# A linear-attention and feed-forward kernel on one core: w to the 128th as one Exp, A in pairs, three quarters of w_in issued together, and a new written-out order

## The chip, the cores and the metric

The kernel runs on one core of one Trainium2 chip. A core has a matrix engine (TensorE, PE in the profile), a vector engine (VectorE, DVE), a scalar engine (ScalarE, ACT), a general engine (GpSimd, POOL) and a queue engine (SyncE, SP) that here only issues DMAs. Each engine runs its own instructions in the order in which they were issued and waits on semaphores for the others. The metric is device time in microseconds (us): 180.36 before, the median of three runs (180.33, 180.36, 181.3).

## The reference

Two layers. The first is a linear attention with a state, over 4 batches, 8 heads, 768 steps and a head size of 48:

```python
for t in range(S):
    cur = einsum('bhd,bhe->bhde', u * k[t], v[t])
    y[t] = einsum('bhd,bhde->bhe', r[t], state + cur)
    state = w * state + einsum('bhd,bhe->bhde', k[t], v[t])
```

w is between 0.85 and 0.95. The second takes x, the y of all heads side by side (3072 rows of 384), through two matrices and a smooth gate:

```python
h = x @ w_in                                   # 384 -> 2048
g = where(h >= 1, h, where(h <= -1, 0, (h + 1)**2 / 4))
out = g @ w_out                                # 2048 -> 384
```

## The kernel before

**Groups.** The 768 steps are cut into 6 chunks of 128. A group g is one chunk of two batches (256 rows of x), so there are 12 groups: g = 0 and 1 are chunk 0 of batches 0,1 and 2,3, and so on. A number n = 2g + j is one batch of a group. Loads of R and K for group 0 are cut into half loads by batch (0.0 and 0.1); the others are whole (384 KB).

**Attention, per group.** Within a chunk the recurrence becomes matrix products. R is scaled by powers of w (`Rs`, line 255), K by inverse powers (`Ks`, 257); `KU` = K u (259), `RKU` = R KU (261), and the sum of RKU over a head is `diag` (274). These four products are named Rs, Ks, KU, RKU with the group's number, the sum usum. V is cast to bf16 (`V`, 140) and `V2` = V diag (279, steps V20.0 and V20.1 for the halves of group 0, V21.0 for group 1 and so on). Per batch: T and TT transpose Rs and Ks on TensorE and copy them out (320, 140; groups 0 to 3), later groups use transposing DMAs (RT, KT, 405). A (331) multiplies them, 8 matmuls with 48 rows each; it takes two of four PSUM banks, and VectorE masks each bank into AT (336, two steps). Y (353, 358) multiplies AT by V and adds the state's part; y (366) adds V2. Sp (343) is the state's new term; Tm (374, 376), decay (379) and sbf (140) bring the state on, with `wCm`, w to the 128th spread over a tile. X and xT transpose y (387, 140; later by DMA, 424).

**Feed-forward, per group.** q runs over four quarters of the 2048 columns. mm1 (459) makes hp = x w_in for a quarter; relu (470 on ScalarE, 472 on VectorE), square (480 on ScalarE, 482 on GpSimd) and gate (489, VectorE) make gt; mm2 (514) multiplies gt by a quarter of w_out into op; o copies op out (140) and out stores it (532). In group 0 a quarter is cut into two halves of 512 columns in three small PSUM buffers; from group 1 on hp has two large ones, in the same banks, which are free once all of group 0's gates are done.

**The powers of w.** ScalarE loads a table for Ln (line 91), takes lw = Ln(w) (146), loads a table for Exp (191); TensorE spreads lw over all partitions (150), and two Exps make the factors Wup and Wdn (166, 169). For wCm, TensorE turns w into a column (wc, 157), VectorE copies it out (174, w_take), GpSimd squares it seven times (178, w_power) and ScalarE spreads it (180, wCm).

**Weights.** w_in and w_out come as four quarters each, cast to bf16 on the way, issued from GpSimd (209); a name with "!" is the issue. The first, w_in0!, is held until R of group 1 has landed, by a one-word copy (208). Everything else is issued by SyncE, on one queue.

**What sets the order.** The program text `PLAN` lists every step once, by name; "/1" takes the second of the engines that the step may run on, "@" gives the PSUM banks, "+n" puts n matmuls ahead of it whose result nobody reads (543, "warm" in the profile). The steps are issued in that order, so each engine runs its own in that order, and GpSimd and SyncE wait in line likewise.

Of the kernel before, what the change touches and what calls it, by code (L numbers as in the profile page):

```python
# [9 lines left out]
F32 = mybir.dt.float32  # L10
# [13 lines left out]
def kernel(  # L24
# [55 lines left out]
    w_col = const.tile([P, NP], F32, name="w_col")  # L80
# [6 lines left out]
    nc.vector.memset(w_col, 1.0)  # L87
# [3 lines left out]
    nc.scalar.preload_act_table_set("natural_log")  # L91
# [33 lines left out]
    FINE = 1  # L125
# [4 lines left out]
    def op(name, where, fn):  # L130
        ops[name] = (where, fn)
# [39 lines left out]
    def w_take(e):  # L171
        for j in range(2):
            rows = slice(j * HP, j * HP + D)
            nc.vector.tensor_copy(w_col[rows, :], tiles["wc"][rows, :])

    def w_power(e):
        for _ in range(C.bit_length() - 1):
            engines[e].tensor_mul(w_col, w_col, w_col)  # L178
# [12 lines left out]
    op("exps", ("ACT",), lambda e: nc.scalar.preload_act_table_set("exp_and_others"))  # L191
    op("Wup", ("ACT",), wup)
    op("Wdn", ("ACT",), wdn)
    op("w_take", ("DVE",), w_take)
    op("w_power", ("POOL", "DVE",), w_power)
# [27 lines left out]
    for g in range(nG):  # L223
# [3 lines left out]
        for j0, j1 in parts:  # L227
# [57 lines left out]
            op(f"V2{tag}", ("POOL", "DVE",) if early_g else ("POOL",), u_term)  # L285
# [23 lines left out]
        for j in range(UNITS):  # L309
# [99 lines left out]
            op(f"A{n}", ("PE",), a_mm)  # L409
# [24 lines left out]
        for q in range(nQ):  # L434
# [6 lines left out]
            for x, (f0, f1) in enumerate(runs):  # L441
# [32 lines left out]
                def square(e, g=g, q=q, x=x, f0=f0, f1=f1):  # L474
# [6 lines left out]
                    elif scale == 1.0:  # L481
                        nc.gpsimd.tensor_mul(sq, pt, pt)  # L482
                    else:
                        nc.gpsimd.scalar_tensor_tensor(out=sq, in0=pt, scalar=0.25, in1=pt, op0=ALU.mult, op1=ALU.mult)
# [17 lines left out]
                op(f"relu {mx}", ("ACT", "DVE",), relu)  # L502
                op(f"square {mx}", ("ACT", "POOL",), square)
# [35 lines left out]
    def fill(n):  # L539
# [9 lines left out]
        RKU0.1/1; load R2.0; X0@3+8; wc@1; Ks1.0/1; xT0; usum0.1; T2@0; w_in1; AT1.1; T3@3; V20.1; TT2; Y1@2; TT3/1; KU1.0;  # L549
        y1; A2@03+3; w_take; X1@2; mm1 (0, 0)00@0; AT2.0; xT1; w_in2; RKU1.0; AT2.1; mm1 (0, 0)01+2; mm1 (0, 1)00@1;  # L550
        relu (0, 0)0/1; mm1 (0, 1)01; mm1 (0, 1)10@2; square (0, 0)0; Sp1@1; V1/1; usum1.0; mm1 (0, 1)11; relu (0, 1)0;
        A3@02; w_in3; Sp0@3; square (0, 1)0; gate (0, 0)0; w_power; relu (0, 1)1; AT3.0; mm1 (0, 2)00@0+5; square (0, 1)1;
        mm1 (0, 2)01; gate (0, 1)0; Y2@0; relu (0, 2)0; mm1 (0, 2)10@1; gate (0, 1)1; load K2.0; mm1 (0, 2)11; AT3.1;
        square (0, 2)0; V21.0; relu (0, 2)1; Y3@2+3; gate (0, 2)0; mm1 (0, 3)00@2; square (0, 2)1; mm1 (0, 0)10@0; y2; wCm;
        mm1 (0, 3)01; Rs2.0; loadV2; gate (0, 2)1; relu (0, 3)0; Tm0; mm1 (0, 3)10@1+5; square (0, 3)0; X2@0; y3;
        mm1 (0, 3)11; mm1 (0, 0)11; Tm1; w_out0!; relu (0, 3)1; load R3.0; Ks2.0/1; relu (0, 0)1; square (0, 3)1; KU2.0;
        gate (0, 3)0; T4@3+12; square (0, 0)1; X3@2; TT4/1; sbf1; load K3.0; xT3; gate (0, 3)1; A4@13+7; xT2; w_out0;
        w_out1!; gate (0, 0)1; T5@2; V2; Sp3@0; RKU2.0; AT4.0; mm1 (1, 0)00; sbf0; Tm3; TT5; AT4.1; Sp2@1; relu (1, 0)0;
        A5@02; Rs3.0; mm1 (1, 1)00; AT5.0; square (1, 0)0; loadV3; AT5.1; w_out1; mm2 (0, 0)0@3; w_out2!; relu (1, 1)0;
        gate (1, 0)0; Y5@0; Y4@2; square (1, 1)0; Ks3.0; usum2.0; mm1 (1, 2)00; Tm2; gate (1, 1)0; relu (1, 2)0; V22.0; T6@1;  # L560
        load R4.0; mm2 (0, 0)1; TT6; w_out2; mm1 (1, 3)00; w_out3!; y4; square (1, 2)0; y5; KU3.0; X4@1; X5@2; mm2 (0, 1)0@0;
        xT4; xT5/1; relu (1, 3)0; gate (1, 2)0; A6@12; mm2 (0, 1)1; V3/1; square (1, 3)0; mm2 (0, 0)2; load K4.0; AT6.0;
        mm1 (2, 0)00; gate (1, 3)0; RKU3.0; w_out3; T7@1; AT6.1; relu (2, 0)0; mm1 (2, 1)00; TT7/1; Rs4.0; square (2, 0)0;
        usum3.0; A7@21; mm2 (0, 1)2; relu (2, 1)0; load R5.0; gate (2, 0)0; V23.0; mm2 (0, 0)3; sbf2; mm2 (0, 1)3; AT7.0;
        square (2, 1)0; mm1 (2, 2)00; AT7.1; Ks4.0; RT4; sbf3; gate (2, 1)0; o (0, 0); Y6@2; o (0, 1); relu (2, 2)0;
        mm2 (1, 0)0@1; loadV4; y6; KU4.0; Y7@3; mm2 (1, 0)1; square (2, 2)0; y7; Sp4@0; Sp5@2; mm1 (2, 3)00; Tm4; RKU4.0;
        KT4; Tm5; gate (2, 2)0; Sp6@3; mm2 (1, 0)2; relu (2, 3)0; xT7; decay4; usum4.0; mm2 (1, 1)0@0; V4; mm2 (1, 0)3;
        decay5; load K5.0; Tm6; square (2, 3)0; mm2 (1, 1)1; o (1, 0)/1; decay6; A8@23; sbf5; mm2 (1, 1)2; sbf4; AT8.0;
        Rs5.0; loadV5; mm1 (3, 0)00; gate (2, 3)0; AT8.1; A9@12; relu (3, 0)0; V24.0; mm1 (3, 1)00; AT9.0; load R6.0;
        square (3, 0)0; AT9.1; Y8@3; Ks5.0; mm2 (1, 1)3; relu (3, 1)0; gate (3, 0)0; Y9@1; RT5; mm2 (2, 0)0@2;  # L570
        square (3, 1)0; KU5.0; y8; mm1 (3, 2)00; y9; V5; KT5; gate (3, 1)0; Sp7@3; Sp8@1; relu (3, 2)0; Rs6.0; mm2 (2, 0)1;
        o (1, 1)/1; xT9; mm1 (3, 3)00; Tm7; square (3, 2)0; Tm8; decay7; load K6.0; mm2 (2, 0)2; gate (3, 2)0; relu (3, 3)0;
        A10@03; decay8; mm2 (2, 0)3; AT10.0; square (3, 3)0; RKU5.0; mm1 (4, 0)00; out (1, 1); AT10.1; sbf6; gate (3, 3)0;
        load R7.0; sbf7; A11@10; relu (4, 0)0; mm2 (2, 1)0@3; usum5.0; Ks6.0; mm1 (4, 1)00; AT11.0; RT6; o (2, 0);
        square (4, 0)0; AT11.1; mm2 (2, 1)1; V25.0; Y10@1; KT6; relu (4, 1)0; gate (4, 0)0; mm2 (2, 1)2; Sp9@2; KU6.0; Y11@0;
        square (4, 1)0; y10; load K7.0; mm1 (4, 2)00; Tm9; y11; gate (4, 1)0; mm2 (2, 1)3; RKU6.0; relu (4, 2)0; Sp10@1;
        xT11; mm2 (3, 0)0@2; Tm10; square (4, 2)0; mm1 (4, 3)00; decay9; usum6.0; loadV6; o (2, 1); mm2 (3, 0)1; Rs7.0;
        gate (4, 2)0; relu (4, 3)0; A12@01; Sp11@3; mm2 (3, 0)2; AT12.0; square (4, 3)0; mm1 (5, 0)00; Ks7.0; AT12.1; RT7;
        gate (4, 3)0; mm2 (3, 0)3; out (0, 1); V6; sbf8/1; Tm11; A13@01; mm1 (5, 1)00; KT7; relu (5, 0)0; sbf9/1; AT13.0;
        AT13.1; decay11; square (5, 0)0; mm2 (3, 1)0@3; loadV7; V26.0; Y13@0; o (3, 0); gate (5, 0)0; mm2 (3, 1)1;  # L580
        relu (5, 1)0; Y12@1; KU7.0; mm2 (3, 1)2; load R8.0; y12; square (5, 1)0; mm1 (5, 2)00; y13; gate (5, 1)0; RKU7.0;
        A14@21; relu (5, 2)0; xT13; mm2 (4, 0)0@0; AT14.0; mm1 (5, 3)00; V7; AT14.1; sbf11/1; load K8.0; usum7.0;
        square (5, 2)0; decay10; mm2 (4, 0)1; relu (5, 3)0; Sp12@2; gate (5, 2)0; mm2 (3, 1)3; Rs8.0; load R9.0; Sp13@1;
        sbf10; mm2 (4, 0)2; o (3, 1)/1; square (5, 3)0; Tm12; mm1 (6, 0)00; V27.0; Tm13; gate (5, 3)0; out (2, 1); A15@32;
        relu (6, 0)0; mm2 (4, 0)3; Ks8.0; RT8; AT15.0; Y14@1; square (6, 0)0; mm1 (6, 1)00; AT15.1; y14; decay12;
# [76 lines left out]
```

## Time and profile before

| | |
|---|---|
| median of three runs | 180.36 us |
| the profiled execution | 179.5 us, its span 177.7 us |
| TensorE busy | 166.5 us (94%) |
| VectorE, ScalarE, GpSimd busy | 139.5, 123.8, 124.6 us |
| DMA, SyncE's queue (q1) | 24.84 MB, 80.5% of 16 engines |
| DMA, GpSimd's queue (q0) | 3.15 MB, 11.6% |
| chain that ended last | PE 77%, of it w_out 35%, w_in 32%, A 3%, Y 4% |

The page gives, per engine, the busy share in 40 slices of the span (4.44 us each), then the chain of work that ended last, followed back from the end: each row is a start, a duration, an engine and a line of the kernel. A row of the timeline has a start, a duration, an engine, a line, and in brackets the idle time before it and what ended that. A row on a DMA queue has the packets, the MB and the share of 16 engines. The clock is TensorE's granted clock; here it is full throughout.

### The profile page before, as it was taken

To read this page: it belongs to the slowest core of one execution; us is meant where nothing else is said; L and a number is where in the kernel's file an instruction comes from. 1 tells how busy PE (TensorE), PEld (TensorE's weight loads), DVE (VectorE), ACT (ScalarE), POOL (GpSimd) and SP (SyncE) were. 2 spreads that over 40 slices of the span, in tenths; PEclk is the share of its full clock that TensorE was granted. 3 is DMA by queue.
4 is the path that set the end of the run, shared out by engine and by line. 5 is a ranking of instruction groups with operands and counts; after the bars stand their busy time and mean duration, and the time that the engine had idled before them with its cause. 6 is when DMAs were issued, how large, how long until landed. Compare 5 with 4: busy or idle time off the path is not lost.

```text
span 177.7 us, 4315 instructions
## 1 busy us (share of the span) xinstructions
PE 166.5 (94%) x1763; PEld 125.3 (70%) x1763; DVE 139.5 (78%) x200; ACT 123.8 (70%) x153; POOL 124.6 (70%) x108
## 2 busy tenths in 40 slices
PE   4997885899999999999999999999999999999992
PEld 4776774787777687786777768777767767776760
DVE  4699889988898889899799878798895698735440
ACT  5453588789796699876987598757776382647852
POOL 2247789949899999899979967997998960040000
PEclk9999999999999999999999999999999999999999
DMA  6999999997989999999999889999989440500104
GB/s 120 192 189 207 194 183 198 219 218 108 212 153 133 204 170 131 253 164 180 232 142 211 190 170 218 195 141 226 149 159 240 121 133 0 130 8 35 53 4 177
DMA packets 105454, 28.28 MB, mean 159 GB/s; under 512 B 98773, under 2 KB 105434, under 8 KB 105434
## 3 DMA queue, kind: packets, MB, share of 16 engines
q1 hardware_dynamic: 101712, 24.84, 80.5%
q0 software_dynamic: 3712, 3.15, 11.6%
q8 instruction: 14, 0.23, 0.6%
q14 instruction: 6, 0.05, 0.1%
q10 hardware_dynamic: 10, 0.01, 0.0%
HBM read 20.45 MB, written 4.72 MB: 142 GB/s over the span
## 4 chain that ended last, share of the span: by engine, by line
PE 77%; DMA 7%; DVE 5%; SPq 4%; POOL 2%; ACT 1%; issue 1%
PE op L514 35%; PE hp L459 32%; DMA VF<-in_v_dram 7%; PE A L331 3%; SPq L237 3%; DVE gt L489 2%; PE Y L358 2%; PE Y L353 2%; PE Sp L343 2%; DVE Ks L257 1%; SPq L297 1%; POOL V L279 1%; POOL w_col L178 1%; ACT sq L480 1%; ACT pt L470 1%
## 5 line engine op out<-in xcount | busy, mean ns | idle before, releaser
L459 PE MATMUL hp<-xT,w_in_sb 128*128 128x256 bf16 (+1 forms) x624 | 71.5, 264 | 1.8 <-DVE gt L489 1.3
L489 DVE SCALAR_TENSOR_TENSOR gt<-sq,hp 128x1024 bf16<-128x1024 f32 (+1 forms) x52 | 58.8, 1133 | 18.4 <-ACT sq L480 16.5
L514 PE MATMUL op<-w_out_sb,gt 128*128 128x384 bf16 x384 | 72.6, 326 | 0.0
L459 PEld LDWEIGHTS <-w_in_sb 128*128 128x128 bf16 x624 | 56.5, 98 | 12.3 <-issue 2.4
L470 ACT ACTIVATE pt<-hp 128x1024 f32<-128x1024 f32 (+1 forms) x49 | 46.9, 960 | 25.3 <-PE hp L459 25.3
L480 ACT ACTIVATE sq<-pt 128x1024 f32<-128x1024 f32 (+1 forms) x51 | 50.4, 991 | 8.1 <-DVE pt L472 6.7
L514 PEld LDWEIGHTS <-gt 128*128 128x128 bf16 x384 | 34.9, 98 | 18.5
L336 DVE TENSOR_TENSOR AT<-A,umask 128x512 bf16<-128x512 f32 x48 | 31.5, 684 | 3.8 <-PE A L331 3.6
L255 POOL TENSOR_TENSOR Rs<-R,Wup 128x768 bf16<-128x768 f32 (+1 forms) x11 | 19.2, 1745 | 5.6 <-ACT Wup L166 4.2
L279 POOL TENSOR_TENSOR V<-V,diag 128x768 f32<-128x768 bf16 (+1 forms) x13 | 17.9, 1375 | 7.3 <-DVE diag L274 4.4
L261 POOL TENSOR_TENSOR RKU<-R,KU 128x768 f32<-128x768 f32 x11 | 20.0, 1819 | 0.4
L259 POOL TENSOR_TENSOR KU<-K,u_bc 128x768 f32<-128x768 f32 x11 | 20.1, 1824 | 0.0
L257 POOL TENSOR_TENSOR Ks<-K,Wdn 128x768 bf16<-128x768 f32 x9 | 16.4, 1822 | 3.3 <-DMA K<-in_k_dram 3.3
L379 POOL TENSOR_TENSOR state<-Tm,wCm 128x384 f32<-128x384 f32 x16 | 16.0, 1003 | 1.3 <-DVE Tm L374 1.3
L366 DVE TENSOR_TENSOR y<-Y,V 128x384 bf16<-128x384 f32 x24 | 12.9, 553 | 3.8 <-PE Y L358 2.6
L274 DVE TENSOR_REDUCE diag<-RKU 128x16 f32<-128x768 f32 (+1 forms) x13 | 11.5, 884 | 1.0 <-POOL RKU L261 0.9
L543 PE MATMUL warm<-ident 128*128 128x128 bf16 x111 | 10.6, 255 | 1.5 <-POOL ident masks.py:199 1.5
L358 PE MATMUL Y<-V,AT 128*128 128x48 bf16 x192 | 11.1, 183 | 0.4 <-DVE AT L336 0.4
L358 PEld LDWEIGHTS <-AT 128*128 128x128 bf16 x192 | 9.7, 96 | 1.5 <-issue 0.7
L482 POOL TENSOR_TENSOR sq<-pt 128x1024 f32<-128x1024 f32 x1 | 1.9, 1892 | 12.5 <-ACT pt L470 12.5
L543 PEld LDWEIGHTS <-ident 128*128 128x128 bf16 x111 | 8.7, 117 | 2.7 <-POOL ident masks.py:199 1.5
L140 ACT COPY o_sb<-op 128x384 f32<-128x384 f32 x15 | 7.0, 475 | 5.0 <-PE op L514 4.4
(67 smaller groups left out, 137.3 us busy)
## 6 DMA issues: line engine op xcount, KB each, us to landing
VF<-in_v_dram SPq DMA_DIRECT2D x12, 384.0 KB, 5.9
R<-in_r_dram SPq DMA_DIRECT2D x11, 384.0 KB, 5.6
K<-in_k_dram SPq DMA_DIRECT2D x11, 384.0 KB, 6.5
out_dram<-o_sb SPq DMA_DIRECT2D x11, 384.0 KB, 2.9
w_in_sb<-in_moe_w_in_dram POOLq DMA_DIRECT2D x4, 384.0 KB, 8.0
w_out_sb<-in_moe_w_out_dram POOLq DMA_DIRECT2D x4, 384.0 KB, 6.6
R<-in_r_dram SPq DMA_DIRECT2D x2, 192.0 KB, 3.6
K<-in_k_dram SPq DMA_DIRECT2D x2, 192.0 KB, 4.2
```

What stands on the lines that cost most here:

```text
L255: engines[e].tensor_mul(part(R_s)[:, :, :, :D], part(R), rep(Wup, j1 - j0))
L259: engines[e].tensor_mul(part(tiles["KU", g]), part(K), rep(u_row, j1 - j0))
L261: engines[e].tensor_mul(part(tiles["RKU", g]), part(R), part(tiles["KU", g]))
L279: engines[e].tensor_mul(tiles["V2", g][:, hs, :], tiles["V", g][:, hs, :], tiles["diag", g][:, hs].unsqueeze(2).to_broadcast([P, n * H, D]),)
L336: nc.vector.tensor_mul(tiles["AT", n][:, i], tiles["A", n][i], umask.unsqueeze(1).to_broadcast([P, NP, P]))
L358: nc.tensor.matmul(Y[:, 2 * p + i, :], AT[:, i, p, :], V[:, j * H + 2 * p + i, :], start=(c == 0), stop=True, skip_group_check=True,)
L459: nc.tensor.matmul(hp[:, f - f0, cols], w_in_sb[:, i, n0 : n0 + P], tiles["xT", g][:, us, i, :], start=(i == 0), stop=(i == nK - 1), skip_ ...
L470: nc.scalar.activation(pt, hp, AF.Relu, bias=0.5, scale=0.5)
L480: nc.scalar.activation(sq, pt, AF.Square, bias=0.0, scale=scale)
L489: nc.vector.scalar_tensor_tensor(out=tiles["gt", g, q][:, f0:f1], in0=tiles["sq", g, q][:, f0:f1], scalar=1.0, in1=tiles["hp", g, q, x], o ...
L514: nc.tensor.matmul(tiles["op", g, j], tiles["gt", g, q][:, f, j * P : (j + 1) * P], w_out_sb[:, n, :], start=(n == 0), stop=(n == nF - 1),)
L543: nc.tensor.matmul(tiles["warm"][:, :P], ident, ident, start=True, stop=True, skip_group_check=True)
```

## The change

- The two table loads become one, of a set that has Ln and Exp. wc is made from lw, not from w, and wCm is Exp(128 lw), two activations that read PSUM. w_take, w_power and the tile w_col are gone.
- From group 6 on (PAIRS = 6) the A of a group's two batches are one step AA on four banks.
- V2 of groups 0 and 1 may run on ScalarE, as eight multiplies a half; one, V20.1, does. relu on VectorE is allowed in groups 0 and 1 alone (none is there now), square on GpSimd from group 2 on.
- PLAN is a new list. The loads start R0.1, R0.0, K0.1, R1, K0.0, V0, K1, R2, K2, V1, V2 (before: R0.0, K0.0, R0.1, K0.1, R1, V0, K1, V1, R2, K2, V2). VectorE makes all products of group 0 and Rs1, Rs2; GpSimd starts with w_in0!, w_in1!, w_in2! and then KU1, V20.0, Ks1, RKU1, w_in3!, w_out0!. Before, it was Rs0.0, w_in0!, w_in1!, V20.0, w_in2!, w_in3!, V20.1, KU1.
- Over the whole: GpSimd has 11 Ks (9 before), 9 Rs (11), 9 casts of V (4), 3 of the state (7) and 5 squares (1); ScalarE has 52 relus (49), 47 squares (51), 4 casts of V (8), 17 of the state (13) and 17 copies o (15). TensorE's products are the same.

```diff
-    nc.scalar.preload_act_table_set("natural_log")
+    nc.scalar.preload_act_table_set("natural_log_exp_and_others")
...
-                    tiles["wc"][j * HP : j * HP + D, p : p + 1], w_row[:, h * D : (h + 1) * D], ones[:, :1],
+                    tiles["wc"][j * HP : j * HP + D, p : p + 1], lw_row[:, h * D : (h + 1) * D], ones[:, :1],
...
-            copy(e, wCm[rows, :, j * D : (j + 1) * D], w_col[rows, :].unsqueeze(2).to_broadcast([D, NP, D]))
+            col = tiles["wc"][rows].unsqueeze(2).to_broadcast([D, NP, D])
+            nc.scalar.activation(wCm[rows, :, j * D : (j + 1) * D], col, AF.Exp, scale=float(C), bias=0.0)
...
+                if e == "ACT":
+                    for h in range(hs.start, hs.stop):
+                        nc.scalar.mul(tiles["V2", g][:, h, :], tiles["V", g][:, h, :], tiles["diag", g][:, h : h + 1])
+                    return
...
-            op(f"A{n}", ("PE",), a_mm)
+            if g < PAIRS:
+                op(f"A{n}", ("PE",), a_mm)
+            elif j == UNITS - 1:
+
+                def aa_mm(e, bank, g=g, f=a_mm):
+                    for y in range(UNITS):
+                        f(e, bank, g * UNITS + y)
+
+                op(f"AA{g}", ("PE",), aa_mm)
...
-        w_row; u_row4; load R0.0; load K0.0; load R0.1; lw_row; exps; lw@0+13; load K0.1; u_bc; load R1.0; Wup; Wdn; Rs0.0;
-        loadV0; Ks0.0/1; Ks0.1/1; T0@1+20; KU0.0/1; TT0; Rs0.1/1; RKU0.0/1; load K1.0; w_in0!; A0@23+10; usum0.0; T1@0;
-        AT0.0; TT1; w_in1!; KU0.1/1; loadV1; Rs1.0/1; V0; A1@12+13; AT0.1; V20.0; AT1.0; Y0@0+10; w_in2!; w_in0; y0; w_in3!;
...
+        w_row; u_row4; load R0.1; load R0.0; load K0.1; lw_row; lw@0+13; load R1.0; u_bc; Wup; KU0.1/1; load K0.0; Wdn;
+        RKU0.1/1; Rs0.0/1; loadV0; Rs1.0/1; w_in0!; Ks0.0/1; w_in1!; load K1.0; KU0.0/1; T0@1+39; w_in2!; Rs0.1/1; RKU0.0/1;
+        TT0; Ks0.1/1; V0; w_in0; usum0.1; T1@2+15; usum0.0; A0@30; V20.1/2; load R2.0; TT1/1; AT0.0; A1@12+5; AT1.0; wc@3;
+        w_in1; KU1.0; AT0.1; wCm; AT1.1; Y0@1+3; Y1@0+1; Sp1@3; Sp0@2; V20.0; w_in2; Ks1.0; y0; y1; X0@1+15; xT0; Tm1;
...
-        Y18@1; mm2 (6, 1)1; decay17; y18; square (8, 1)0; loadV10; mm1 (8, 2)00; sbf15/1; Tm18; gate (8, 1)0; KU10.0;
-        mm2 (6, 1)2; relu (8, 2)0; A20@31; Y19@2; AT20.0; square (8, 2)0; mm2 (6, 1)3; decay16; y19; mm1 (8, 3)00;
...
+        mm2 (7, 0)3; Tm18; loadV11; V210.0; Tm19; mm1 (9, 0)00; o (7, 0); gate (8, 3)0; o (7, 1); sbf16; Rs11.0; AA10@3012;
+        relu (9, 0)0; mm1 (9, 1)00; AT20.0; square (9, 0)0; AT20.1; KU11.0; RT11; mm2 (8, 0)0@3; AT21.0; sbf17; relu (9, 1)0;
```

More of the change, by code (lines that the diff above doesn't have):

```diff
@@ L123 @@
     u_row = u_bc.rearrange("p (h d) -> p h d", h=H)
-    FINE = 1
+    FINE, PAIRS = 1, 6
     FLEX, XDMA, TDMA, VCAST = 3, 3, 4, 12
@@ L550 @@
[L550 to L583, printed above, removed]
@@ new lines @@
+        mm1 (0, 0)10@1+5; square (0, 1)1; Ks2.0; A2@01; loadV2; mm1 (0, 0)11; relu (0, 2)0; gate (0, 1)1; w_in3; A3@23;
+        relu (0, 0)1; AT2.0; mm1 (0, 2)10@2; square (0, 2)0; mm1 (0, 2)11; AT3.0; KU2.0; square (0, 0)1; T4@0; gate (0, 2)0;
+        relu (0, 2)1; gate (0, 0)1; w_out0; square (0, 2)1; V1/1; AT2.1; mm1 (0, 3)00@0+12; TT4; AT3.1; mm1 (0, 3)01; V21.0;
+        Y2@2; gate (0, 2)1; mm1 (0, 3)10@1; relu (0, 3)0; mm1 (0, 3)11; square (0, 3)0; Y3@1; RKU2.0; y2; relu (0, 3)1; y3;
+        X2@0+5; square (0, 3)1; load R3.0; gate (0, 3)0; X3@3+1; A4@21; xT3; w_out1!; gate (0, 3)1; xT2; T5@3; sbf1; AT4.0;
@@ L625 @@
         if fn:
-            engine = where[1 if other else 0]
+            engine = where[int(other[1:]) if other else 0]
             indices = iter(slots[1:] if slots else "")
```

115 lines of the change are left out of this document (64 added, 51 removed).

## The prediction

> **What bounds the kernel now.** I read the page's slices first, then the chain of waits, then the opening engine by engine, then the DMA queues in short windows. The slices:
>
> ```profile
> PE   4997885899999999999999999999999999999992
> PEclk9999999999999999999999999999999999999999
> DMA  6999999997989999999999889999989440500104
> ```
>
> TensorE is full from the eighth slice on, at full clock; before that it is not. The chain of waits says where the opening hands over:
>
> ```profile
> 8.81 13.20 DMA VF<-in_v_dram
> ...
> 28.72 2.62 DVE Ks L257
> ...
> 32.54 1.20 DVE gt L489 x2
> ...
> 33.79 1.50 PE hp L459 x12
> ...
> 59.69 1.31 PE hp L459 x12
> 61.00 0.33 PE A L331 x8
> 61.33 1.42 PE hp L459 x12
> ...
> 169.05 5.21 PE op L514 x32
> 174.29 0.48 ACT o_sb L140
> ```
>
> From 33.79, the first w_in matmul of group 1, TensorE runs with hardly a gap to 174.26. My check, by chain rows: 44 w_in steps x 1.31 = 57.7, 96 w_out steps x 0.65 = 62.4, 19 A x 0.44 (0.33 and a dearer follower, below) = 8.4, 20 Y x 0.38 = 7.6, the rest about 4: 140.1 of 140.47 us. No order can shorten that stretch but by removing work. The tail (174.26 to 177.7: copy, store) is unchanged in the new plan. So the time is: when does the first w_in matmul of group 1 start, what does A cost, does anything new stall.
>
> The same fence shows A's price: the w_in step that starts at 61.33, behind an A, takes 1.42 instead of the 1.31 of the step at 59.69. The same 0.11 stands behind nearly every A.
>
> In the opening ScalarE works off group 0's sixteen half steps without a pause worth naming, at 0.61 + 0.54 = 1.15 us a pair:
>
> ```profile
> 20.22 0.63 ACT L480 ACTIVATE sq<-pt 128x512 f32<-128x512 f32 x1 [1.31 <-DVE pt L472]
> 20.76 0.58 ACT L470 ACTIVATE pt<-hp 128x512 f32<-128x512 f32 x1
> 21.37 0.63 ACT L480 ACTIVATE sq<-pt 128x512 f32<-128x512 f32 x1
> ```
>
> Last, the DMA queues (q1 is SyncE's, q0 GpSimd's). First 14 to 14.75 us, between the first and second w_in quarter; then 18 to 22, inside the third and fourth:
>
> ```profile
> q1 hardware_dynamic: 779, 0.15, 99.0%
> ...
> q0 software_dynamic: 654, 0.65, 95.9%
> q1 hardware_dynamic: 629, 0.12, 25.9%
> ```
>
> In the pause SyncE's queue moves about 1,000 packets a us, as before w_in; under w_in it gets 157, one for each w_in packet. A load of 384 KB is 2,048 packets, so w_in nearly stops the loads.
>
> **The change, part by part.**
>
> *Removed on ScalarE and GpSimd.* The second table load (1.28), w_take (0.32 on VectorE), w_power (1.86 on GpSimd from 22.85). The table load is worth nothing: Wup waits for TensorE's lw to 5.48 anyway (0.43 idle before it). w_power lay on the chain between V1's cast and V2 of group 1; it goes, but what is late next there is the loads, below. In its place wCm is two Exps of 48x192: between 0.34 (the copy of that shape) and 0.58 (Exp of 128x384); I take 0.34, the same shape. V20.1 becomes eight ScalarE multiplies of 128x48: between 0.14 each (VectorE's 128x1 row) and 0.34 (wCm's copy); midway, 0.25, 2 us. ScalarE is idle between V0 (done 12.4) and xT0 (19.2), so both are hidden; were they not, 2.7 us would be at stake.
>
> *The opening.* The four half loads landed at 3.64, 5.16, 6.17 and 7.2, R1 behind them, so that three whole loads were through, at 9.32. In the new order R1 ends two and a half: 8.25. GpSimd copies a word of it (0.18), and w_in0 is issued at 8.45 instead of 9.47, w_in1 and w_in2 right behind. The first w_in packets moved 2.28 us after the issue (9.47 to 11.75): now 10.73.
>
> VectorE makes all products of group 0 and Rs1: KU0.1 at 6.2, RKU0.1, Rs0.0, wait for R1, Rs1 8.25 to 9.2, then Ks0.0, KU0.0, Rs0.1, RKU0.0, Ks0.1 at 0.47 each (done 11.8), two sums (12.75), TT1 (13.4), four AT at 0.64 (15.95). y0 ran at 13.94 before; on this engine alone it is 2 us later.
>
> y0 also needs V20.0, which now stands on GpSimd behind KU1, so behind the load of K1. K1 is packet 10,240 of SyncE's queue. At 10.73 about 9,055 are through (9,225 by 10.9). w_in0 takes 2.2 us (340 of q1 moved in such a window, 11.75 to 13.95), the pause gives 779, 66 are left: 0.4 us at 157. The count is full at 14.1; V0 and R1 landed 1.55 after theirs: K1 lands at 15.7. In the window of w_in0 the near row is mixed: its first quarter still belongs to the loads, and from 12.5 to 13.75 q1 moved next to nothing. Taken that way, 190 packets, K1 lands at 16.7.
>
> The Trainium skill ("DMA: Bandwidth & Descriptors", Queues, rings and completion order) says that each engine round-robins between queue rows by packet; the 18 to 22 window, 654 against 629, agrees. By that rule q1 keeps its 340 and the sum stands; by the empty quarters it would be 1.0 us worse.
>
> I take 15.7, nearest to three of the four w_in windows. Then KU1 to 17.5 (1.80), V20.0 to 18.3 (0.82), y0 and y1 to 19.3 (0.55, pitch 0.47), X1 and xT1 to 20.2, first relu at 20.75. ScalarE's stream is then: 8 pairs x 1.15 = 9.2, sbf0 0.5, TT3 and TT4 0.95 each, 11.6 in all, to 32.35; last gate 0.67, so group 1 starts at 33.1. Before: 33.79. xT3, xT2, sbf1, TT5 (2.4) follow on ScalarE, so relu (1,0) is at 34.65 against 35.31. **Gain 0.65.**
>
> What must not be later than that stream: the loads behind K1. w_in1 and w_in2 end at 19.05 with some 11,400 packets through; from there, free, q1 moves 1,125 a us (2,250 from 23 to 25): R2 and K2 (packets 12,288 and 14,336) land at 21.4 and 23.3, V1 (16,384) at 25.2. So V1, moved behind R2 and K2, is 3 us later than its 22.0, and what it feeds is due later still. w_in3 is issued behind KU1, V20.0, Ks1 and RKU1 on GpSimd at 21.9, lands 5.8 later (w_in0's row), 27.7, and its relu is due at 29.95. GpSimd: w_in3, w_out0 to 23.45, Ks2 25.2, KU2 27.0, V1's cast 27.8, V21.0 29.25; y2, y3 to 30.3; X3 and xT3 before 32. So 1 to 2 us of cover each.
>
> *A in pairs.* For groups 6 to 11, 12 A become 6 pairs: 6 followers save 0.11 = 0.66. A pair takes all four banks, and its four AT (0.64 each) can stand before a gate. I worked the six pairs from their rows: gate (6,1), behind three AT, ends 3.8 us after its pair starts, and mm1 (6,3) wants it at 3.7: 0.2 us lost. The others have 0.1 to 1 us left, and the copies of the two op banks that a pair needs end some 0.7 us before it. **Gain 0.45**; ends: no exit cost saved and all stalls doubled (minus 0.4), or 0.66.
>
> *GpSimd after the opening.* Five more casts (+4.1), two more Ks (+3.6), two fewer Rs (-2.8), four fewer state casts (-2.0), V20.1 (-0.8), one square among them (+1.9): 4 us more on an engine whose V2 of group 11 ended at 145.3, where y22 ran at 152.3. GpSimd is also ahead: Ks4 done at 47 instead of 51.4. So covered; without that cover each us late is a us at A or y. The three squares among the last (1.89 instead of 1.06) leave gate (11,2) 0.8 us before its w_out step, by the rows of the steps between. ScalarE gains and loses within 2 us at 70% busy: relus +3, state casts +4, o +2, squares -4, V casts -4; nothing on TensorE waits for it after the opening. SyncE carries the same 76 DMAs; the transposes of group 4 on have some 5 us before their A. out (0,1) now stands before xT9; it waits for o (0,1), some 10 us earlier in the order. w_out1 to w_out3, issued from 31 on, land 37.5 to 43.5, wanted at 40 to 46.
>
> Sum: 179.5 (span 177.7 and 1.8 around it) - 0.65 - 0.45 = 178.4. That execution stands 0.86 below the median of the runs; against the median 180.36 it is **179.3**, 0.6% less. A run of this kernel can tell some 0.5% (0.9 us) from nothing.
>
> **Rivals.**
>
> 1. *The gain is eaten* (26%). K1 at 16.7, or no exit cost saved: gain 0.1 to 0.65, 179.7 to 180.3. Or the port between VectorE and GpSimd: Ks2 on VectorE took 2.70 where alone it takes 0.95, beside KU2 on GpSimd. Now Rs2 (VectorE, from 22.9) meets Ks2 (GpSimd, from 23.45). VectorE is first by 0.5 us; if it is second, two gates are 1.7 late and ScalarE loses about 1.4: 180.7. The Trainium skill ("SBUF — State Buffer", SBUF: two separate sides) calls that an exclusive lock that goes to whichever starts first; the 2.70 agrees.
>
> 2. *Three quarters in one go close the pause* (12%, slower). w_in2 and w_in3, queued together, ran without one. If w_in1 follows w_in0 so, K1 has 845 packets to go at 157: full at 18.4, landing at 19.9, everything behind V20.0 4.2 later: 183.5. It decides from a pause under 0.5 us (K1 after 16.8). Against it: w_in1 was queued 0.9 us behind w_in0 before too, and the 0.75 pause was there.
>
> 3. *The pairs stall* (16%, slower). If at each pair a gate is one AT later than I worked out, uncovered, 0.64 x 6 = 3.8 is lost against 0.65 and 0.66: 182.9. For it: only two hp buffers. Against: the margins above, thin but there.
>
> 4. *The opening is shorter than I think* (12%). If K1 lands as w_in starts (14.0), AT1.1 at 15.95 and KU1 bound y0 at 16.6: 1.7 more, 177.6.
>
> **Chances.** My forecast holds 34%, rival 4 12%: faster 46%. Rival 1 is same, 26%; 2 and 3 slower, 28%. The range 177.5 to 182.9 takes in 4, 1 and 3 and leaves out most of 2. The likeliest case's own is 178.4 to 179.5.
>
> **What will show it.** In the new profile: GpSimd's KU1 starts at 15.7 on K1's landing (not 13.5, not 20); first relu 20.75; ScalarE without gaps to the last square; group 1's first w_in matmul at 33.1; behind each pair one dearer follower, not two; TensorE full after. Gaps there at a gate, or KU1 after 17, make me wrong.

## The result, and the profile after

The changed kernel takes **178.8 us** (median of 20 runs, 177.29 to 180.09) against 180.87 for the kernel before, measured beside it (20 runs, 178.93 to 182.71): a ratio of 0.989, 95% interval 0.986 to 0.992, so 1.1% faster. Each ratio in this document compares a kernel's faster runs with those of the kernel before taken beside them, so it isn't quite the quotient of the two medians. The forecast was 179.3 with a range of 177.5 to 182.9. The changed kernel's profiled execution took 178.9, with a span of 177.0. That is only 0.6 to 0.7 less than the profiled execution of before (179.5 and 177.7), while the medians lie 2.07 apart; where the rest is, the experiments show.

The slices of the kernel after:

```profile
PE   4997984899999999999999999999999999999992
PEclk9999999699999999999999999999999999999999
DMA  5999999999473997978997997999958350070014
```

TensorE is full from the eighth slice on, as before, but in that slice its granted clock is down. The chain of waits (start, duration, what):

```profile
10.38 12.29 DMA K<-in_k_dram
...
22.75 1.82 POOL Ks L244
24.56 1.80 POOL KU L246
26.36 2.18 issue
28.57 0.83 POOL V L138
...
29.47 1.49 POOL V L270
30.98 0.57 DVE y L357
...
34.14 1.66 PE hp L459 x12
...
86.66 1.31 PE hp L459 x12
87.97 0.55 PE A L322 x16
88.52 1.42 PE hp L459 x12
...
167.74 5.86 PE op L512 x36
173.62 0.48 ACT o_sb L138
```

Two things differ. Before, the chain of the opening ran through the load of V1 (landed at 22.0); now it runs through the load of K2 and then to the cast of V1 at 28.57, and GpSimd stands still ahead of that cast. And a pair of A's is one piece of 0.55, not two of 0.33. The chain's first w_in step after that opening takes 1.66 instead of the 1.31 of a later one.

The opening in the timeline of the kernel after, engine by engine (start, duration, engine, line, operation; in brackets how long the engine stood idle before it, and for what):

```profile
12.29 1.80 POOL L246 TENSOR_TENSOR KU<-K,u_bc 128x768 f32<-128x768 f32 x1 [1.13 <-DMA K<-in_k_dram]
...
18.39 0.60 ACT L470 ACTIVATE pt<-hp 128x512 f32<-128x512 f32 x1 [0.58 <-PE hp L459]
...
28.57 0.82 POOL L138 CAST V<-VF 128x768 bf16<-128x768 f32 x1 [2.20 <-DMA VF<-in_v_dram]
...
29.44 0.36 PE L349 MATMUL Y<-V,AT 128*128 128x48 bf16 x8 [2.42 <-POOL V L138]
...
30.51 0.60 ACT L470 ACTIVATE pt<-hp 128x512 f32<-128x512 f32 x1 [1.51 <-PE hp L459]
...
30.98 1.02 DVE L357 TENSOR_TENSOR y<-Y,V 128x384 bf16<-128x384 f32 x2 [2.53 <-POOL V L270]
...
33.93 1.87 PE L459 MATMUL hp<-xT,w_in_sb 128*128 128x256 bf16 x12
```

KU1 starts at 12.29, not at 15.7, and ScalarE's first relu at 18.39, not at 20.75: the front of the opening is 2.4 us better than forecast. Then V1 arrives 3.3 us later than forecast (28.5 instead of 25.2), TensorE, ScalarE and VectorE all stand idle for it, and group 1's first w_in step starts at 33.93, where before had 33.79 and the forecast 33.1. Why V1 was late is seen in the DMA queues of the kernel after, window 22 to 25 (queue, packets, MB, share):

```profile
q0 software_dynamic: 646, 0.55, 118.3%
q1 hardware_dynamic: 127, 0.02, 6.1%
```

GpSimd had come to its issues of w_in3 and w_out0 already at 18.36 and 19.16 (forecast 21.9), because KU1 was early. In 22 to 25 those two transfers move, and SyncE's queue, with V1 behind K2 in it, moves 127 packets; by single microseconds 38, none and 89. In the same window before, it moved 2,933.

The idle time had a second price. Busy time by stretch of the kernel after (from and to, length, then the busy time of PE, PEld, VectorE, ScalarE and GpSimd with their instructions, then the granted clock, the DMA share and GB/s):

```profile
28.00:30.00 2.00, 0.56 (x15) 0.56 (x15) 0.45 (x1) 0.97 (x2) 1.35 (x2) 1.00 0.99 199
30.00:32.00 2.00, 1.36 (x26) 1.12 (x23) 1.02 (x3) 1.23 (x2) 2.00 (x2) 0.83 1.22 242
32.00:34.00 2.00, 1.97 (x22) 1.55 (x21) 2.00 (x4) 1.27 (x3) 2.00 (x3) 0.50 1.25 224
34.00:36.00 2.00, 2.00 (x22) 1.45 (x19) 1.28 (x2) 1.17 (x2) 1.99 (x4) 0.82 1.02 116
```

TensorE was busy for 0.56 of the 2 us from 28, and from about 31.3 to 34.7 it runs at a clock of 0.50: two groups of four T matmuls follow each other at 0.38 to 0.42 instead of 0.23, and the w_in step lasts 1.81 from start to start instead of 1.31, together some 0.8 us. It isn't a thing of the profiled execution alone: one stretch of 3.4 us at 0.50 lowers the mean clock of an execution by 0.01, and 19 of the changed kernel's 20 runs have a mean of 0.991 or less, against 16 of the 46 runs of the kernel before beside the experiments.

So the opening gave nothing in this pair of profiles, and the gain lies behind it. From the third w_in step of group 1 to TensorE's end both kernels do the same matmuls: before from 38.73 to 174.25, 135.5 us; after from 39.26 to 173.58, 134.3. That is 1.2 less, where the forecast had 0.45.

### The profile page after: what moved, and what is told of

Read it like the earlier page. It is cut to its first block, busy times and chain, and to the rows that moved or that the text cites. A ratio compares the mean times of both kernels' runs of the same rounds, so it can differ in the third digit from the quotient of the medians.

```text
span 177.0 us, 4328 instructions
## 1 busy us (share of the span) xinstructions
PE 166.2 (94%) x1770; PEld 127.3 (72%) x1770; DVE 132.4 (75%) x191; ACT 123.1 (70%) x161; POOL 133.5 (75%) x105
## 4 chain that ended last, share of the span: by engine, by line
PE 77%; DMA 7%; SPq 5%; POOL 3%; issue 2%; DVE 2%; ACT 1%; POOLq 0%
PE op L512 34%; PE hp L459 32%; DMA K<-in_k_dram 7%; SPq L224 5%; PE A L322 3%; PE Y L349 2%; PE Y L344 2%; PE Sp L334 2%; PE T L311 1%; POOL Ks L244 1%; POOL KU L246 1%; POOL V L270 1%; DVE gt L487 1%; SPq L288 1%; PE X L378 1%
## 5 line engine op out<-in xcount | busy, mean ns | idle before, releaser
L512 PE MATMUL op<-w_out_sb,gt 128*128 128x384 bf16 x384 | 70.3, 326 | 0.0
L470 ACT ACTIVATE pt<-hp 128x1024 f32<-128x1024 f32 (+1 forms) x52 | 49.7, 956 | 27.6 <-PE hp L459 26.7
L512 PEld LDWEIGHTS <-gt 128*128 128x128 bf16 x384 | 35.8, 98 | 19.6
L480 ACT ACTIVATE sq<-pt 128x1024 f32<-128x1024 f32 (+1 forms) x47 | 46.2, 986 | 1.3
L244 POOL TENSOR_TENSOR Ks<-K,Wdn 128x768 bf16<-128x768 f32 x11 | 20.0, 1821 | 5.2 <-DMA K<-in_k_dram 4.7
L482 POOL TENSOR_TENSOR sq<-pt 128x1024 f32<-128x1024 f32 x5 | 9.5, 1893 | 14.4 <-ACT pt L470 9.8
L242 POOL TENSOR_TENSOR Rs<-R,Wup 128x768 bf16<-128x768 f32 x9 | 16.4, 1823 | 0.0
L138 ACT COPY o_sb<-op 128x384 f32<-128x384 f32 x17 | 8.0, 474 | 8.4 <-PE op L512 7.4
L541 PE MATMUL warm<-ident 128*128 128x128 bf16 x118 | 11.7, 265 | 1.5 <-POOL ident masks.py:199 1.5
L541 PEld LDWEIGHTS <-ident 128*128 128x128 bf16 x118 | 9.7, 123 | 2.7 <-POOL ident masks.py:199 1.5
```

The source lines that it names most:

```text
L244: engines[e].tensor_mul(part(K_s)[:, :, :, :D], part(K), rep(Wdn, j1 - j0))
L470: nc.scalar.activation(pt, hp, AF.Relu, bias=0.5, scale=0.5)
L480: nc.scalar.activation(sq, pt, AF.Square, bias=0.0, scale=scale)
L512: nc.tensor.matmul(tiles["op", g, j], tiles["gt", g, q][:, f, j * P : (j + 1) * P], w_out_sb[:, n, :], start=(n == 0), stop=(n == nF - 1),)
L541: nc.tensor.matmul(tiles["warm"][:, :P], ident, ident, start=True, stop=True, skip_group_check=True)
```

## The experiments

### One Exp alone, and the kernel before again

The first theory of the prediction to test was the "nothing" at the removal of w_power. One kernel has that part of the change alone, in the order of before:

```
-    op("exps", ("ACT",), ...)
-    op("w_take", ("DVE",), w_take)
-    op("w_power", ("POOL", "DVE",), w_power)
     op("wCm", ("ACT",), w_spread)      # w_spread as in the change: two Exps
-        ... V1/1; usum1.0; ... gate (0, 0)0; w_power; ... AT3.1; square (0, 2)0; V21.0; ...
+        ... V1/1; usum1.0; ... gate (0, 0)0; ... AT3.1; square (0, 2)0; V21.0; ...
         # w_take goes too, and wCm stands where w_take stood
```

> The kernel before with one part of the change alone: one table load, w's logarithm straight from PSUM through two Exps into wCm, no w_take and no w_power; the order, the A one by one and everything else are those of before. Theory 'covered' (the prediction's term of nothing): ScalarE's table load goes (1.28) and GpSimd's w_power (1.86 from about 22.9), but w_power's place is taken by waiting for the next load, so V21.0, y2 and y3 come at most 0.3 earlier, group 1's first w_in matmul stays at 33.5 to 33.9 (before 33.79), and the time is the one of before within 0.3%. Rival 'on the path': w_power stood between V1's cast and V21.0; without it V21.0 ends about 1.9 us earlier, the first w_in matmul of group 1 starts at 32 to 33, and the time falls by 0.5 to 1%.

178.72 us (178.13 to 179.47, 4 runs) against 180.56, ratio 0.987 (0.983 to 0.992): on its own this part is worth as much as the whole change. To see why the profiles showed so little of it, the kernel before was profiled twice more.

> The kernel before, unchanged, for a second profile: its runs have a median of 180.9, its profiled execution had 179.5 (V1's cast at 22.06, group 1's first w_in matmul at 33.79, 140.5 from there to TensorE's end). Theory 'V1's landing': in an execution of 180 or more V1's cast comes later than 22.06, and w_power, V21.0, y2, y3 and the first w_in matmul of group 1 come later by the same time (34.3 to 35.2), with the 140.5 behind it unchanged. Rival 'the stretch behind': V1 at 22 and the first w_in matmul at 33.8 as before, but 141 to 142 from there to TensorE's end (waits or a clock below 0.99). If this execution is again one of about 179.5, it shows 33.6 to 34.0 and tells nothing of the two.

> The kernel before once more, for a third profile; the same two theories and the same numbers as for the second: V1's cast and group 1's first w_in matmul later by the same time and 140.5 unchanged, or 33.8 unchanged and the stretch behind it 141 to 142.

These executions took 181.68 and 180.72. The second profile of before, GpSimd and the first w_in step of group 1:

```profile
23.97 0.82 POOL L140 CAST V<-VF 128x768 bf16<-128x768 f32 x1 [3.77 <-DMA VF<-in_v_dram]
24.76 1.85 POOL L178 TENSOR_TENSOR w_col<-w_col 128x4 f32<-128x4 f32 x7
26.56 1.48 POOL L279 TENSOR_TENSOR V<-V,diag 128x768 f32<-128x768 bf16 x1
...
35.71 1.48 PE L459 MATMUL hp<-xT,w_in_sb 128*128 128x256 bf16 x12
```

The third profile of before:

```profile
22.95 0.82 POOL L140 CAST V<-VF 128x768 bf16<-128x768 f32 x1 [2.74 <-DMA VF<-in_v_dram]
...
34.67 1.48 PE L459 MATMUL hp<-xT,w_in_sb 128*128 128x256 bf16 x12
```

And the kernel with one Exp alone:

```profile
23.09 0.82 POOL L138 CAST V<-VF 128x768 bf16<-128x768 f32 x1 [2.84 <-DMA VF<-in_v_dram]
23.99 1.48 POOL L270 TENSOR_TENSOR V<-V,diag 128x768 f32<-128x768 bf16 x1
...
33.13 1.48 PE L459 MATMUL hp<-xT,w_in_sb 128*128 128x256 bf16 x12
```

In three executions of before V1's cast starts at 22.06, 22.95 and 23.97, and group 1's first w_in step at 33.79, 34.67 and 35.71: 0.89 and 1.02 of delay come through as 0.88 and 1.04. From there to TensorE's end it is 140.5, 140.8 and 140.7. So V1's cast, w_power, V21.0 and y2 were the path that set the end of the opening, and V1's landing makes nearly all of the spread of these three. The execution that the prediction was built on was one with an early V1. With V1 at 23.09 and without w_power the step starts at 33.13: against the third profile of before, with V1 0.14 earlier, that is 1.54 less, so 1.7 at the same landing, which is w_power's 1.86 nearly in full. (On the way y2 comes 1.56 earlier, VectorE then loses 0.36 of it in a wait for a square of ScalarE, and its Ks2 beside GpSimd's KU2 takes 2.35 here against 2.70, which makes that up again.) So with V1 at 23 us the theory "covered" falls. With an earlier V1 it holds in part: in the kernel of the next section that has before's opening and one Exp, V1's cast runs at 20.92, yet y2 starts only at 25.59, behind a gate on VectorE, and GpSimd's Rs2 waits 2.52 for its load. In before, with V1 at 22.06 and w_power, y2 started at 26.17. So with so early a V1 w_power is worth some 0.6 there, an estimate from these two rows.

### The old opening with the new order behind it, and the reverse

```
     # open_before: before's steps up to mm1 (1, 0) (with one Exp, Sp3 later), then the changed order
     # open_after: the changed order up to mm1 (1, 0), then before's steps, every A by itself
```

> All steps up to the first w_in matmul of group 1 in the order of the kernel before (with one Exp; wCm right behind wc, where w_take stood, since it now reads the bank), Sp3 left to its later place; all the rest in the new order, pairs included. Theory 'steady': the new opening is worth nothing (group 1 began at 33.93 in the new profile, at 33.79 in the old one) and the gain lies behind it, so this is as fast as the changed kernel: ratio to before 0.985 to 0.993. Theory 'opening': the profiled run is not typical and most of the 2 us lie in the opening: ratio 0.994 to 1.000.

> The reverse: the new order up to the first w_in matmul of group 1, then the remaining steps in the order of before, A not paired. Theory 'steady': ratio to before 0.997 to 1.003, group 1 beginning near 34. Theory 'opening': 0.987 to 0.993.

With before's opening: 177.46 us (6 runs) against 180.88, ratio 0.986 (0.981 to 0.992). With the new opening and before's order behind it: 180.98 (12 runs), ratio 1.002 (0.998 to 1.007). Two comparisons are clear. With before's order behind it, exchanging the old opening for the new one takes the kernel with one Exp from 0.987 to 1.002, a loss of 1.5%. Behind the new opening, exchanging before's order for the new one with its pairs goes from 1.002 to 0.989, a gain of 1.3%. Behind the old opening the new order's gain is 1.3 us by medians (178.72 to 177.46, on two chips) but hardly any by ratio (0.987 to 0.986), with intervals that hold both. There the trace is clearer: from group 1's third w_in step to TensorE's end the kernel with before's opening and the new order takes 134.6 (39.42 to 174.05), the one with one Exp and before's order 135.6. So the new order gains 1.0 us behind the old opening too, and the parts don't simply add up: what the new opening costs is 1.5% in front of before's order and 1.3 us by medians, but only 0.3% by ratio with intervals that overlap, in front of the new one. The changed kernel's gain is the one Exp and the order behind; its new opening adds nothing and takes a part of it away, by an amount that isn't settled. In the reversed kernel V1 is late as in the changed one:

```profile
28.30 0.82 POOL L138 CAST V<-VF 128x768 bf16<-128x768 f32 x1 [2.28 <-DMA VF<-in_v_dram]
```

and the clock falls there too (0.57, 0.50, 0.50 and 0.72 in the stretches from 30 to 38).

### The pairs taken apart

The pairs can be taken apart in two ways. In one, the second A goes behind the w_in step that follows the pair:

```
-        ... sbf9; AA6@1023; relu (5, 1)0; mm1 (5, 2)00; ...
+        ... sbf9; A12@10; relu (5, 1)0; mm1 (5, 2)00; A13@23; ...      # so for all six
```

> The changed kernel with each pair taken apart: the second A stands behind the w_in step that followed the pair, everything else in place. If a pair saves one dearer follower (0.11 us, six times), this is 0.66 us slower than the changed kernel: ratio to before about 0.993, and twelve dearer followers in the profile from group 6 on. Rival: the pair saves nothing, because the second A's end costs what the first's did or the burst of four AT costs as much: 0.989 or less.

182.53 us (6 runs), ratio 1.012 (1.006 to 1.018): some 4 us more than the changed kernel, far above the expected 0.66. Its timeline shows why this run doesn't price the pair alone. The order of everything else is made for pairs, and the copies of a later A hold up what follows. From group 1's third w_in step to TensorE's end it takes 137.4, 3.1 more than the changed kernel; six A's more in runs of their own are some 1.3 of that (by the price found below), and the rest is waits such as the last of these rows, not all of them accounted for:

```profile
100.44 1.48 PE L459 MATMUL hp<-xT,w_in_sb 128*128 128x256 bf16 x12 [0.32 <-DVE gt L487]
101.86 0.40 PE L322 MATMUL A<-RT,KT 48*128 48x128 bf16 x8
...
103.63 0.20 PE L349 MATMUL Y<-V,AT 128*128 128x48 bf16 x1 [0.38 <-DVE AT L327]
```

In the other way the first A of four pairs goes ahead of the step before the pair, so that nothing is later than it was:

```
-        ... o (3, 0)/1; mm1 (5, 1)00; ... sbf9; AA6@1023; relu (5, 1)0; ...
+        ... o (3, 0)/1; A12@10; mm1 (5, 1)00; ... sbf9; A13@23; relu (5, 1)0; ...   # so for 6, 9, 10, 11
```

> The changed kernel with four of its six pairs (groups 6, 9, 10, 11) taken apart again: the first A of each is moved ahead of the w_in step that stood before the pair, the second stays; the copies behind them and all else stay where they are. Theory 'a run of A's costs 0.10 us when it is entered and 0.11 when it is left': 16 runs instead of 12, each of the four steps ahead of a moved A is about 0.10 longer from start to start, each single A lasts 0.33 where the pair of two lasted 0.55; by the stretch from group 1 to TensorE's end 4 x 0.21 = 0.84 us more than the changed kernel, +0.5%, with no new stall above 0.2. Rival 'only the step behind is dearer, 0.11 each' (the prediction's price): +0.44 us, 0.25%. Rival 'the pairs are worth nothing and unpaired lost its time by stalls alone': within 0.1 us of the changed kernel.

179.5 us (12 runs), ratio 0.9945 (0.991 to 0.998): 0.7 us by median and 0.6% by ratio above the changed kernel. The times can't tell 0.84 from 0.44; the trace can. The chain of waits of this kernel, at group 6:

```profile
86.06 0.33 PE A L322 x8
86.39 1.42 PE hp L459 x12
87.81 0.33 PE A L322 x8
88.14 1.42 PE hp L459 x12
```

Two A's by themselves cost 2 x (0.33 + 0.11 for the dearer follower) = 0.88; the pair in the chain of the changed kernel, shown above, 0.55 + 0.11 = 0.66. A pair saves 0.22, not 0.11: the second A of a pair costs 0.22, since it has neither a dearer follower nor an entry of its own. From group 1's third w_in step to TensorE's end this kernel needs 135.57, 1.25 more than the changed one: four times 0.21, and 0.41 lost at the A of group 9, whose bank VectorE's Tm had not yet read.

### w_out0 later, and V1 first

```
-        ... Tm0; w_out0!; mm1 (0, 1)11; ...      # late_wout0
+        ... V21.0; w_out0!; Y2@2; ...
```

> The changed kernel with one step moved: the issue of w_out0 goes behind V2 of group 1 on GpSimd. In the new profile w_in3 and w_out0 move from 21.3 to 26 us, and the load of V1, behind K2 on the other queue, lands only at 28.57; the y of group 1 wait for it. Theory 'starved': without w_out0 in that stretch V1 lands 1 to 2.5 us earlier and group 1 begins at 31.5 to 33: ratio to before 0.976 to 0.984. Rival 'place': V1 is late because R2 and K2 stand before it and the loads are what they are: 0.987 to 0.991, V1 landing after 28.

178.0 us (176.16 to 181.19, 6 runs), ratio 0.980 (0.974 to 0.987). In its profiled execution (178.92, above its median), with w_in3 alone in GpSimd's queue, SyncE's queue moved 1,912 packets in 22 to 25, where the changed kernel's moved 127. This holds across the runs. In the four profiles with w_out0 issued right behind w_in3 (the changed kernel's, the two with its A's apart, and the reversed one) SyncE's queue moved 90 to 479 packets in that window and V1 landed at 28.25 to 28.84; in the three with w_out0 later it moved 1,870 to 1,944. V1 landed at 26.39 here, 2.1 us earlier than in the changed kernel. But K2 came later, as in one of those four as well (Ks2 at 24.97), and GpSimd's order then put V1 behind it:

```profile
24.85 1.81 POOL L244 TENSOR_TENSOR Ks<-K,Wdn 128x768 bf16<-128x768 f32 x1 [5.96 <-DMA K<-in_k_dram]
26.63 1.81 POOL L246 TENSOR_TENSOR KU<-K,u_bc 128x768 f32<-128x768 f32 x1
28.40 0.82 POOL L138 CAST V<-VF 128x768 bf16<-128x768 f32 x1
...
33.24 1.47 PE L459 MATMUL hp<-xT,w_in_sb 128*128 128x256 bf16 x12
```

V1's cast has no wait of its own any more, and is still at 28.40. The step starts 0.7 earlier than in the changed kernel, and the clock stays up. So with w_out0's transfer out of the way V1 is no longer what is waited for, and the order on GpSimd (Ks2, KU2, then V1) is the next bound, 0.2 us behind it. The next kernel turns that order round as well:

```
-        ... load K2.0; ... loadV1; ... Ks2.0; ... KU2.0; ... V1/1; ... V21.0; ...      # v1_first
+        ... loadV1; load K2.0; ... V1/1; V21.0; Ks2.0; ... KU2.0; w_out0!; ...        # T4, A4 later
```

> The changed kernel with V of group 1 put first: its load ahead of K2 on SyncE's queue, its cast and V21.0 ahead of Ks2 and KU2 on GpSimd, w_out0's issue behind KU2, T4 behind X3 on TensorE, A4 behind the first w_in step of group 1. Theory 'V1 held the end of the opening': V1's cast runs at 22.5 to 25.5 instead of 28.57, y2 and y3 at 26 to 29 instead of 30.98, ScalarE keeps its stream, group 1's first w_in matmul starts at 31.3 to 32.5 instead of 33.93, the time is 1 to 2 us under the changed kernel (0.6 to 1.1%). Rival 'something else is due at the same time' (K2 through Ks2 and T4, w_in's last quarter at 27, or the clock): the first w_in matmul of group 1 not before 33.2, less than 0.6 us gained.

179.32 us (6 runs), ratio 0.990 (0.986 to 0.994): nothing gained. The timeline of its profiled execution, its longest (181.9):

```profile
26.18 0.82 POOL L138 CAST V<-VF 128x768 bf16<-128x768 f32 x1 [7.39 <-DVE gt L487]
...
31.08 1.47 PE L459 MATMUL hp<-xT,w_in_sb 128*128 128x256 bf16 x12
...
36.20 0.84 POOL L138 CAST V<-VF 128x768 bf16<-128x768 f32 x1
```

The opening is 2.85 us shorter, as the theory said, with V1 only 2.4 earlier. It is given back at once: the Y of group 2 waits for V2's cast, which stood behind KU2, RKU2 and three issues of w_out until 36.20. TensorE stands idle for 2.63 us, and its clock goes down to 0.50 from about 35.1 to 41.9. From its first w_in step of group 1 to TensorE's end this execution needs 145.6 instead of 139.65. The median of its six runs is 2.6 us below this execution, so the others lost less; how much of it behind the opening, no profile shows. One more step moves V2's cast ahead of RKU2 and KU2 to VectorE:

```
-        V21.0; Ks2.0; ... KU2.0; w_out0!; ... RKU2.0; ... w_out1!; ... w_out2!; ... V2/1;
+        V21.0; Ks2.0; w_out0!; ... gate (0, 3)1; V2/1; KU2.0/1; RKU2.0; w_out1!; w_out2!;      # v1_fix
```

> The kernel with V of group 1 put first (there the first w_in matmul of group 1 started at 31.08, 2.85 before the changed kernel's 33.93, but then TensorE waited 2.8 us at the Y of groups 4 and 5 for V2's cast, which stood on GpSimd behind KU2, RKU2 and three issues of w_out, and its clock fell to 0.50 from 36 to 41.5). Now V2's cast stands ahead of RKU2, KU2 is made by VectorE behind the last gate of group 0, and w_out0 is issued behind Ks2. Theory 'the opening's gain is real once nothing behind it waits': V2's cast at 31 to 33, no wait of TensorE over 1 us between 31 and 42, clock at full there, TensorE's end at 171 to 172.5, the time 2 to 3 us under the changed kernel (1.1 to 1.7%, ratio to before 0.972 to 0.980). Rival 'the supply of group 1 and 2 cannot follow': a new wait of the same size at y4, at w_out's first quarter or at A, and no more than 0.7 us gained on the changed kernel.

178.25 us (177.34 to 179.61, 6 runs), ratio 0.983 (0.978 to 0.988): 0.5 better than the changed kernel by median, where 2 to 3 was expected. Group 1's first w_in step is at 31.51 and TensorE's end at 173.82, 142.3 apart. The long wait is gone, smaller ones are there, the largest at w_out's first quarter:

```profile
41.31 0.81 PE L512 MATMUL op<-w_out_sb,gt 128*128 128x384 bf16 x4 [1.00 <-DMA w_out_sb<-in_moe_w_out_dram]
```

Here the rival was right in the number, and not in its form: no single wait of the old size came back, but what stands behind the opening isn't there earlier, so most of an opening made shorter by loads and issues moved round is lost again in several smaller waits. Part of the difference is the clock: it is at 0.50 in this execution too, for 3.4 us from 14.9, inside the opening.

### The port in the old opening

```
-        ... Rs2.0; ... Ks2.0/1; ...        # open_before: Rs on GpSimd, Ks on VectorE
+        ... Rs2.0/1; ... Ks2.0; ...        # ob_ks2
```

> The kernel with before's opening and the new order behind it (177.5 profiled), and in group 2 VectorE makes Rs and GpSimd Ks, where it was the other way round. Theory 'the port': Ks of group 2 took 3.09 on VectorE at 28.13 because GpSimd ran KU beside it; T4, X3 and the last two gates stood behind it. Now Rs on VectorE takes 0.95 to 1.1 at about 26, before GpSimd's Ks begins; Ks on GpSimd takes 1.82 and ends at 29.5 to 30, the gates come 1 to 1.5 us earlier, group 1's first w_in matmul starts at 32.6 to 33.2 instead of 34.07, and the time falls by 0.9 to 1.5 us (0.5 to 0.8%) against the same kernel without it. Rival 'K of group 2 lands too late anyway': Ks on GpSimd begins only at 29 and ends at 31 as before, gain under 0.3 us. Rival 'the product is slow for another reason': Rs on VectorE takes over 2 us too.

The fastest by median: 177.35 us (176.68 to 178.75, 6 runs), ratio 0.980 (0.976 to 0.984). The timeline of the kernel with before's opening and Ks2 on VectorE:

```profile
28.13 3.09 DVE L244 TENSOR_TENSOR Ks<-K,Wdn 128x768 bf16<-128x768 f32 x1
28.58 1.82 POOL L246 TENSOR_TENSOR KU<-K,u_bc 128x768 f32<-128x768 f32 x1
```

and of the one with the two exchanged:

```profile
26.06 0.96 DVE L242 TENSOR_TENSOR Rs<-R,Wup 128x768 bf16<-128x768 f32 x1 [0.52 <-DMA R<-in_r_dram]
27.46 1.81 POOL L244 TENSOR_TENSOR Ks<-K,Wdn 128x768 bf16<-128x768 f32 x1 [2.39 <-DMA K<-in_k_dram]
...
32.18 1.47 PE L459 MATMUL hp<-xT,w_in_sb 128*128 128x256 bf16 x12
```

A product of VectorE that ends before GpSimd's begins takes 0.96; one with GpSimd's KU2 beside it takes 3.09 and ends 0.82 after KU2 does. The Trainium skill ("SBUF — State Buffer", SBUF: two separate sides) calls it a lock that goes to whichever starts first, while the other fully blocks. That VectorE's product isn't through until GpSimd's is agrees, with 0.82 behind it here and 0.82 to 0.83 in the profiles of before; that the first to start has it is not what these rows show, since Ks2 is shown as starting 0.45 ahead of KU2. The first w_in step is 1.9 earlier than the 34.07 of the kernel without the exchange. But in that kernel's profiled execution, its slowest of six, TensorE waited 2.18 us for that Ks2 and the clock fell to 0.50 for 3.4 us, which its mean clock shows in none of the other five runs; the medians of the two (on different chips) are 0.1 apart, and the ratios 0.6%. That the product is fast this way round is shown, what it is worth in the time is not settled.

## Why the prediction was right or wrong

**The sign and the time were right**, 178.8 against 179.3, but two of the terms were wrong in size and one in place, and they partly cancelled.

**"Removed": w_power at nothing.** Wrong. The prediction saw that it lay between V1's cast and V21.0 and gave it up because "what is late next there is the loads". With V1 at 23 us its removal was worth 1.7 us in before's order. The loads were not late there: Rs2, KU2 and Ks2 simply followed V21.0 and y2. With a V1 as early as in the execution that the prediction went by, the loads are indeed next, after some 0.6 (an estimate, above). The step that failed was to drop a duration that lies on the path without timing the load that should have covered it. In the changed kernel V1 is so late that w_power's place isn't even reached, so this gain is there only against the lateness that the new opening brings.

**The opening: gain 0.65.** Its front was better than worked out (KU1 at 12.29 instead of 15.7, first relu 18.39 instead of 20.75): SyncE's queue had moved 9,949 packets by 11 us where the sum, by the count of before, took 9,225 by 10.9, and K1's last packets had moved by 11.26, with w_in's first only at 11.16. Its end was worse. The prediction gave V1 the landing of 25.2 and the issue of w_in3 21.9; an early KU1 brought the issues of w_in3 and w_out0 to 18.36 and 19.16, just ahead of V1's packets, and V1 landed at 28.5. "1 to 2 us of cover each" was gone, with TensorE idle 2.4 and then 0.8 lost to a slow clock, some of it behind the first w_in step. Against the profiled execution of before the opening lost 0.14; against the third profile of before (34.67) it gained 0.74 there. By the third w_in step, with the slow clock in, it has lost 0.53 against the former (39.26 and 38.73). Rival 2 named the mechanism, GpSimd's transfers stopping a load, but for K1 and w_in1, and there it didn't happen; rival 4's early K1 happened, without its gain.

**The queues.** The sum shared packets one to one between the queues while GpSimd's had work, and took SyncE's queue as undisturbed until w_in3's transfer, issued at 21.9 in the sum. With w_in3 and w_out0 issued some 3 us earlier, V1's packets fell into a stretch that was shared, and shared at 646 to 127 in 22 to 25 us. The rule of the Trainium skill cited in the prediction ("DMA: Bandwidth & Descriptors", Queues, rings and completion order: turns by packet) doesn't describe that stretch, counted in the profile's packets; the measurement decides. In the prediction's own view, 12.5 to 13.75 in before, SyncE's queue had moved next to nothing as well. The prediction set that window aside for the three that fitted, and so had no price for it.

**A in pairs: 0.45.** The mechanism was right, the term 0.66 was half of what it is: 0.21 to 0.22 a pair, 1.3 for six, because the second A of a pair costs 0.22 and not 0.33. The stall foreseen at the pair of group 7 (0.2) is there: the w_in step behind that pair starts 0.16 late, for gate (6, 0) and not for gate (6, 1). 1.3 less 0.16 is some 1.1 of the 1.2 us that the steady part gained.

**Hidden work, GpSimd, the tail.** Right. The two Exps of wCm took 0.65 together (0.68 in the sum), V20.1 1.91 (2.0), both unseen; Rs2 took 0.96 beside nothing, so rival 1's port didn't bind; behind the opening no step of TensorE waits for GpSimd or a load.

**From one execution to the median.** The prediction carried before's 0.86 between profile and median over to the new kernel. In two of three profiles of before V1 landed later than in the one it went by, so most of that difference looks like V1 landing late in most executions; the runs without a profile don't show it. The changed kernel's path has its own bound: its profiled execution is at its median (178.9 and 178.8). Of the 2.07 us between the medians, 0.6 is in the two profiles; the rest is of the size of the 0.9 and 1.9 by which V1 came later in the two further profiles of before.

That the time came out so near owes something to chance. The sum by the profile, 178.4, was 0.5 too low, and the 0.86 added on top made 179.3, 0.5 too high.

## What to carry to other kernels

An operation that stands on the path is worth its duration unless the thing said to be late next has a time of its own; write that time down before costing the removal at nothing, and for more than one execution: here the same removal was worth 1.7 us with a late load and some 0.6, by an estimate, with an early one. When an early step pulls forward the issue of large transfers, look at which small load stands behind them, not only at the step. And before a sum is carried to a median, profile the same kernel more than once: the difference between executions can be one load's landing on the path.

## What the runs showed of the hardware

Two transfers of GpSimd's queue at work together left SyncE's queue 38, 0 and 89 packets in three successive microseconds, and 90 to 479 in the same three microseconds of three more kernels; with one at work (w_out0 issued later) it moved 1,870 to 1,944 there, in three kernels. From 16 to 18, with w_in1 and w_in2 issued one behind the other, the queues went about even, 319 to 318. What decides between the two was not settled.

One and the same load, issued within 0.2 us of the same time, landed between 22.0 and 23.9 in three executions of one kernel.

In five executions a wait of TensorE of 2.1 to 2.5 us in the opening was followed by a granted clock of 0.50. It began 0.2 to 1.9 us after the engine was busy again (1.9 in the changed kernel) and lasted 3.4 us, 6.8 in the reversed kernel. In the kernel with V1 first it fell during a wait of 2.6 us, for 6.8. Single waits of up to 1.8 us in the three profiles of before were not followed by a fall. The length of one wait doesn't decide it alone: in the last of the kernels with V1 first the clock fell at 14.9 us behind several waits of 0.2 to 0.4. A long wait of TensorE was dearer by that than its length.

A run of 48-row A matmuls costs 0.33 for eight and 0.55 for sixteen, and makes the step behind it 0.11 longer once a run, not once an A.
